# A hand-written order for a sort-attention kernel that feeds a maxout FFN: paired value sorts, groups of three PSUM tiles, other places for the loads

## The chip, the cores and the metric

The kernel runs on one core of one Trainium2 chip. The metric is the device time of one execution in microseconds (us), taken as the median of several runs. Times within one execution are read from a hardware profile of that execution, counted from its first instruction.

The engines are named as in the profile: PE is TensorE (matmuls; PEld its weight loads), DVE is VectorE, ACT is ScalarE, POOL is GpSimd, SP is SyncE. In this kernel POOL starts the loads from memory and SP starts the transposing DMAs and nearly all stores.

## The reference, cut to what matters

There are four items (B = 4), each with 8 heads, 768 positions and a head size of 64. The positions form 8 blocks of 96. An 8 by 8 matrix P for each item and head, made from `sort_net` by five Sinkhorn rounds, mixes the blocks of k and of v; attention then runs inside each block, and a maxout FFN follows on all 512 columns.

```python
for _ in range(5):                       # Sinkhorn
    P = exp(P - max(P, -1)); P /= sum(P, -1); P /= sum(P, -2)
k_sorted = einsum('bhij,bhjcd->bhicd', P, k_b)   # v_sorted alike
attn = softmax(scale * q_b @ k_sorted_b.T)       # within each block
x = (attn @ v_sorted_b)                          # -> (4*768, 8*64)
out = maximum(x @ w1, x @ w2) @ w_out            # (3072, 512), fp32
```

The maxout is computed as `relu(x (w1 - w2)) w_out + x (w2 w_out)`. So `w1` is replaced by the difference (four pieces, `w_difference`), and the product `wc = w2 w_out` is made once (`w2_transposes`, `w_product`). Once the differences are taken and w2 is transposed, w2 itself is not read any more.

## The kernel before, in words

Items are counted from one in this text (item one is `b = 0` in the code), steps within an item from 0.

**PSUM.** There is one pool of four tiles, each 128 x 1024 fp32 [...]. Every product of every kind takes a tile from it: `k_ps`, `v_ps`, `s_ps`, `o_ps`, `h_ps`, `out_ps`, `tq_ps`, `wc_ps`. A tile is handed out again when the instruction that reads it last has run, so a matmul group may have to wait for a copy on ACT or DVE.

**Steps of an item.** `load_k`, `load_v`, `load_q` (lines 132 to 161) start casting DMAs on POOL; each load instruction also waits for the landing of the eighth one before it. k and q come in buffers `k_raw` (two) and `q_raw` (one); v of two items lies in one buffer `v_raw`, one item in partitions 0 to 63 and the other in 64 to 127. `turn_v` reorders v into `v_dc`. `block_diagonals` spreads P into block-diagonal weights `bd`. Then:

- `sort_k(b, t)`, t = 0 to 2: 32 matmuls of 64 rows each into one PSUM tile, copied to `kT`.
- `sort_v(b, t)`, t = 0 to 3: 16 matmuls of 64 rows of one item, copied to `v_sb`. `sort_v_pair(b, t)`, t = 0 to 7: 16 matmuls, 8 for each of two items that lie in the two halves of the partitions; with this, two items take 8 tiles.
- `q_transposes`: item one and two by PE; later items are first laid in pairs (`pair_q`, DVE) and then transposed by two DMAs that SP issues.
- `scores(b, u)`, u = 0 to 7: 8 matmuls into one tile, then exp on ACT into one of 8 buffers `e`. u = 0, 1, 4, 5 need the first half of the transposed q, the others the second.
- `values(b, u)`: 8 matmuls of `e` with `v_sb`, then on DVE a reciprocal and a product that gives x.
- `x_transposes(b, t)`, t = 0 to 3, one for each two values steps: by PE for item one, by a DMA from SP (`xT`) for the others.

**The FFN of an item** is a list of units: 8 times `moe_h` (8 matmuls of 384 columns, then relu on ACT or DVE; the first four read transposes 0 and 1 of x, the last four 2 and 3), for item one 4 times `w_product`, and 12 times half an output tile (`moe_out`, 6 matmuls of 512 columns; four of them fill a PSUM tile, which is then copied and stored by SP).

**The order.** The program order of each engine is the order in which the Python code emits instructions. The start, to the end of item one's attention, is written by hand (lines 666 to 716), with matmuls on zeros (`keep_streaming`) at places where PE would stand still. In the loop (lines 743 to 805) the attention of item b+1 is woven into the units of item b: a dictionary `tail` gives some steps by hand, and the rest (`steps`) is spread evenly by the units' costs in the list `cost`. `pick` chooses ACT or DVE for a copy by a running estimate of their load.

Values are sorted so: item one alone, item two alone (`sort_v`), items three and four as a pair (`sort_v_pair`) in the FFN of item two. Scores are emitted in groups of two. The loads stand in the order v1 k1 q1 weights v2 k2, then (after three FFN units) q2 k3, later v3 v4 k4, q3, and q4 after q3 is laid in pairs.

Of the kernel before, what the change touches and what calls it, by code (L numbers as in the profile page):

```python
# [10 lines left out]
FP32 = mybir.dt.float32  # L11
BF16 = mybir.dt.bfloat16
# [4 lines left out]
def kernel(  # L17
# [112 lines left out]
        e_bufs.append(t)  # L130

    def load_q(b, by_pair=False):
        t = qpool.tile([128, H, R * D], BF16, tag="q_raw", name="q_raw", bufs=1)
        src = q[b].rearrange("h (p r) d -> p h (r d)", r=R)
        for hs in [slice(hp, H, HP) for hp in range(HP)] if by_pair else [slice(0, H)]:
            nc.gpsimd.dma_start(out=t[:, hs], in_=src[:, hs])  # L136
        q_raw[b] = t
# [13 lines left out]
                in_=k_src[b, :, ci * n : (ci + 1) * n],  # L151
            )

    def load_v(b, c0=0, pieces=2):
        r0 = (b % 2) * 64
        n = (BLK - c0) * D // pieces
        for m in range(pieces):
            nc.gpsimd.dma_start(
                out=v_raw[r0 : r0 + 64, c0 * D + m * n : c0 * D + (m + 1) * n],
                in_=v_src[b, :, c0 * D + m * n : c0 * D + (m + 1) * n],  # L160
            )

    w1_sb = big.tile([128, HP, DFF], BF16, tag="w1", name="w1_sb")
# [13 lines left out]
        c = slice(t0 * DFF // 4, t1 * DFF // 4)  # L177
        nc.gpsimd.dma_start(out=dst[:, :, c], in_=s[:, :, c])

    load_v(0, 0, 3)  # L180
    ident = const.tile([128, 128], BF16, tag="ident", name="ident")
    make_identity(nc, ident)
    load_k(0)
# [18 lines left out]

    w_difference(0, nc.gpsimd)
    w_difference(1, nc.gpsimd)
    load_v(1)
    load_k(1)


# [42 lines left out]


    id64 = const.tile([128, 64], FP32, tag="id64", name="id64")
    maskJ = const.tile([128, 6, NB], FP32, tag="maskJ", name="maskJ")
    maskM = const.tile([128, 2, 8], FP32, tag="maskM", name="maskM")

    def masks(part):
# [21 lines left out]
    sel_v, sel_k = {}, {}  # L279

    def selections(b):
        src = ident[0:G, b * 8 : b * 8 + 8]
        if b % 2 == 0:
            sel_v[b] = const.tile([G, 16, NB], BF16, tag=f"sel_v{b}", name="sel_v")
            nc.vector.tensor_copy(
                out=sel_v[b], in_=ident[0:G, b * 8 : b * 8 + 16].to_broadcast([G, 16, NB])
            )
        sel_k[b] = const.tile([G, 8, 16], BF16, tag=f"sel_k{b}", name="sel_k")
        nc.vector.tensor_copy(out=sel_k[b], in_=src.to_broadcast([G, 8, 16]))

    bd_v, bd_k = {}, {}

    def block_diagonals(kinds, m0=0):

        pe = ps_f32("pe")
        n = len(kinds)
        for c, (m, b) in enumerate(kinds):
            sel = (
                sel_k[b].rearrange("g h w -> g (h w)")
                if m  # L300
                else sel_v[b].rearrange("g h j -> g (h j)")
            )
            nc.tensor.matmul(
                pe[:, c * 64 : c * 64 + 64],
                sel,
                p_bf.rearrange("p i j -> p (i j)"),
                start=True,
                stop=True,
            )
        pm = const.tile([128, n, NB, NB], FP32, tag=f"pm{n}", name="pm")  # L310
        nc.vector.tensor_tensor(
            out=pm,
            in0=pe[:, 0 : n * 64].rearrange("p (m i j) -> p m i j", i=NB, j=NB),
            in1=maskJ[:, m0 : m0 + n].to_broadcast([128, n, NB, NB]).transpose([0, 1, 3, 2]),
            op=ALU.mult,
        )
        pt = const.tile([128, n, NB], FP32, tag=f"pt{n}", name="pt")
        nc.vector.reduce_sum(out=pt, in_=pm, axis=AX.X)
        for c, (m, b) in reversed(list(enumerate(kinds))):
            bd = const.tile([128, 8, NB], BF16, tag=f"bd{m}{b}", name="bd")  # L320
            nc.vector.tensor_tensor(
                out=bd,
                in0=maskM[:, m].to_broadcast([128, 8, NB]),
                in1=pt[:, c].to_broadcast([128, NB, 8]).transpose([0, 2, 1]),
                op=ALU.mult,
            )
            if m:
                bd_k[b] = bd.rearrange("p m i -> p (m i)")
            else:
                bd_v[b] = bd_v[b + 1] = bd.rearrange("p m i -> p (m i)")  # L330


    v_sb = big.tile([BLK, 128, D + 16], BF16, tag="v_sb", name="v_sb")
# [15 lines left out]
    def q_transposes(b, half, eng=None):  # L349
# [8 lines left out]
            )  # L358
            return
        ps = ps_bf16("tq_ps")  # L360
        if b == 0:
            nc.tensor.matmul(
                ps[:, 0:128], fill[:, 0:128], ident, is_transpose=True, start=True, stop=True
            )
# [44 lines left out]
    def sort_v(b, t, n=0, eng=None):  # L409
# [3 lines left out]
        for m in range(16):  # L413
# [8 lines left out]
        evac(  # L422
            v_sb[:, m0 : m0 + 64, t * 16 : (t + 1) * 16],
            ps[0:BLK].rearrange("p (d m) -> p m d", m=64),
            1024,
            eng=eng,
        )
# [235 lines left out]
        return SC, VA, TR  # L663

    first, second, both = slice(0, 64), slice(64, 128), slice(0, 128)
    keep_streaming(ps_f32("fill_ps"), 88 * 138, most=138)
    for it in range(5):
        sinkhorn(it)
        if it < 2:
# [9 lines left out]
    turn_v(first, "D", 80, 96)  # L679

    SC, VA, TR = att(0)
    sort_k(0, 0, 2048, "A")
    sort_k(0, 1, 0, "D")
    sort_k(0, 2, 0, "A")
    sort_v(0, 0, 0, "D")
# [2 lines left out]
    sort_v(0, 2, 0, "A")  # L688
    sort_v(0, 3, 0, "D")
    SC[0]()  # L690
    SC[1]()
    q_transposes(0, 1, "D")
    SC[4]()
    VA[0]()
    scores(0, 2, 1024)
    VA[1]()
    SC[3]()
    values(0, 2, 1024)
    x_transposes(0, 0, "A")
    values(0, 3, 512)  # L700
    SC[5]()
    moe_h_products(0, 0, 0, (0, 2), 512)
    x_transposes(0, 1, "A")
    VA[4]()
    SC[6]()
    moe_h(0, 0, 0, "A", (1, 3))
    SC[7]()
    VA[5]()
    moe_h(0, 0, 1, "A")
    x_transposes(0, 2, "A")  # L710
    VA[6]()
    w_difference(2)
    VA[7]()
    w2_transposes(0, "D")()
    w_difference(3)
    for b in range(1, B):
        selections(b)
    for c, n, m in [(2, 1, 0), (3, 3, 1)]:
        nc.vector.tensor_copy(
            out=maskJ[:, c : c + n],  # L720
            in_=maskJ[:, m].to_broadcast([128, NB, n]).transpose([0, 2, 1]),
        )
# [2 lines left out]
        turn_v(rows, "D", c0, c0 + 24)  # L725
        load["D"] += 850

    def load_rest():
        load_q(1)
        load_k(2)  # L730

    tail = {
        2: [TR[3], lambda: w2_transposes(1, "A")(), load_rest],
        4: [lambda: turn(second, 0)],
        5: [lambda: block_diagonals([(0, 2), (1, 1), (1, 2), (1, 3)], 2)],
        6: [lambda: turn(second, 24), lambda: turn(second, 48)],
        7: [lambda: turn(second, 72)],
        8: [lambda t=t: sort_k(1, t) for t in range(3)],
        9: [lambda: load_v(2), lambda: load_v(3), lambda: load_k(3)],
        14: [lambda: load_q(2)],  # L740
        18: [lambda: pair_q(2, 0), lambda: pair_q(2, 1), lambda: load_q(3)],
    }
    for b in range(B):
        units = [lambda t=t: moe_h(b, 0, t, None if b else "A") for t in range(4)]
        if b == 0:
# [13 lines left out]
        if b == B - 1:  # L759
# [1 line left out]
                lambda: moe_out_last(4, [(0, 512, "D")]),  # L761
                lambda: moe_out_last(5, [(0, 384, "D"), (384, 512, "A")]),
            ]
        steps, lo = [], 0
        if b < B - 1:
            qs = [lambda half=half: q_transposes(b + 1, half) for half in range(2)]
            ks = [lambda t=t, b=b: sort_k(b + 1, t) for t in range(3)]
            SC, VA, TR = att(b + 1)

            def group(*fs):  # L770
                return [lambda: [f() for f in fs]]

            if b == 0:
                lo = 9
                vs = [lambda t=t: sort_v(1, t) for t in range(4)]
                for m, c in enumerate((0, 24, 48, 72)):
                    VA[m + 1 : m + 2] = group(VA[m + 1], lambda c=c: turn(both, c))
                steps = group(*vs[0:2]) + group(vs[2], qs[0]) + group(vs[3], qs[1])
            elif b == 1:
                vs = [lambda t=t: sort_v_pair(2, t) for t in range(8)]  # L780
                tail[0] = qs
                tail[10] = [lambda: pair_q(3, 0), lambda: pair_q(3, 1)]
                steps = group(*ks) + group(*vs[0:2]) + group(*vs[2:4]) + group(*vs[4:6])
                steps += group(*vs[6:8])
            else:
                tail[0] = qs
                lo = 4
                steps = group(*ks)
            steps += group(*SC[0:2]) + VA[0:1] + group(*SC[2:4]) + VA[1:2] + group(VA[2], TR[0])
            steps += group(*SC[4:6]) + VA[3:4] + group(VA[4], TR[1]) + group(*SC[6:8]) + VA[5:6]  # L790
            steps += group(VA[6], TR[2]) + group(VA[7], TR[3])
        done = 0
        for n, unit in enumerate(units):
            elapse(100 * cost[n] if n < len(cost) else 0)
            unit()
            for step in tail.get(n, []):
                elapse(250)
                step()
            total = sum(cost[lo:])
            want = -(-len(steps) * sum(cost[lo : n + 1]) // total)  # L800
            while done < min(want, len(steps)):
                elapse(250)
                steps[done]()
                done += 1
        tail = {}
# [1 line left out]
_INS = ['q', 'k', 'v', 'sort_net', 'moe_w1', 'moe_w2', 'moe_w_out']  # L807
_OUTS = [((3072, 512), 'float32')]
# [25 lines left out]
```

## Time and profile before

| | |
|---|---|
| median of 5 runs | 170.65 us (170.15 to 171.35) |
| profiled execution | 170.15 us |
| its span, first to last instruction | 168.3 us |
| granted PE clock | 0.999 of full |
| PE busy | 160.7 us, 2000 matmuls |
| ACT busy / DVE busy | 85.7 us / 75.8 us |
| moved by DMA | 23.11 MB, mean 137 GB/s |
| largest groups | output products (line 617) 47.0 and 24.8 us; FFN products (590) 44.7 us; exp (469) 24.3 us |

Busy times of PE overlap, since matmuls are pipelined: a group's mean of 370 ns for 512 columns is longer than its share of the chain, in which consecutive ones take about 0.21 us each. A line of section 5 of the page gives the idle time ahead of a group and what ended it; a line of the chain in order of time gives start, length and what ran. Line 108 and 110 are the copy helper on ACT and DVE, line 82 the matmuls on zeros.

### The profile page before, as it was taken

To read this page: it belongs to the slowest core of one execution; us is meant where nothing else is said; L and a number is where in the kernel's file an instruction comes from. 1 tells how busy PE (TensorE), PEld (TensorE's weight loads), DVE (VectorE), ACT (ScalarE), POOL (GpSimd) and SP (SyncE) were. 2 spreads that over 40 slices of the span, in tenths; PEclk is the share of its full clock that TensorE was granted. 3 is DMA by queue.
4 is the path that set the end of the run, shared out by engine and by line. 5 is a ranking of instruction groups with operands and counts; after the bars stand their busy time and mean duration, and the time that the engine had idled before them with its cause. 6 is when DMAs were issued, how large, how long until landed. Compare 5 with 4: busy or idle time off the path is not lost.

```text
span 168.3 us, 4526 instructions
## 1 busy us (share of the span) xinstructions
PE 160.7 (96%) x2000; PEld 96.8 (58%) x2018; DVE 75.8 (45%) x174; ACT 85.7 (51%) x104; POOL 28.9 (17%) x44
## 2 busy tenths in 40 slices
PE   7999999999999999999999999999999999999991
PEld 7839667655764454566664545557545455654451
DVE  5978874957454458537734434205443160000011
ACT  3587878465673354176674504457605406642020
POOL 7857496233212004000000000000000000000000
PEclk9999999999999999999999999999999999999999
DMA  3999999999999994999700344590053255000333
GB/s 43 204 204 199 199 207 206 224 198 206 213 217 206 205 245 79 191 152 225 161 0 4 91 127 143 104 285 5 0 51 125 58 166 171 0 0 0 125 143 110
DMA packets 30243, 23.11 MB, mean 137 GB/s; under 512 B 16720, under 2 KB 25168, under 8 KB 30224
## 3 DMA queue, kind: packets, MB, share of 16 engines
q0 software_dynamic: 10880, 12.59, 44.7%
q1 hardware_dynamic: 19200, 10.17, 25.0%
q8 instruction: 16, 0.26, 0.6%
q10 hardware_dynamic: 144, 0.07, 0.1%
q14 instruction: 3, 0.02, 0.0%
HBM read 25.17 MB, written 6.29 MB: 187 GB/s over the span
## 4 chain that ended last, share of the span: by engine, by line
PE 86%; DVE 7%; issue 2%; ACT 2%; DMA 1%
PE out_ps L617 36%; PE h_ps L590 26%; PE o_ps L488 4%; PE wc_ps L570 4%; PE k_ps L394 4%; PE s_ps L461 4%; PE v_ps L415 2%; PE tq_ps L369 2%; PE v_ps L436 1%; DMA p_sb<-in_sort_net_dram 1%; PE tx_ps L526 1%; DVE colsum L243 1%; DVE p_sb L240 1%; ACT v_sb L108 1%; DVE rowsum L239 1%
## 5 line engine op out<-in xcount | busy, mean ns | idle before, releaser
L617 PE MATMUL out_ps<-wo_sb,g 128*128 128x512 bf16 (+2 forms) x188 | 47.0, 370 | 1.1 <-issue 0.3
L590 PE MATMUL h_ps<-xT,w_sb 128*128 128x384 bf16 x256 | 44.7, 326 | 0.6 <-ACT xT L108 0.4
L590 PEld LDWEIGHTS <-w_sb 128*128 128x128 bf16 x256 | 24.0, 98 | 16.4 <-DVE w_sb L194 0.4
L108 ACT COPY o<-out_ps 128x1024 f32<-128x1024 f32 x11 | 11.1, 1012 | 40.4 <-issue 22.8
L604 ACT ACTIVATE g<-h_ps 128x768 bf16<-128x768 f32 x27 | 21.9, 811 | 16.5 <-PE h_ps L590 16.5
L469 ACT ACTIVATE e<-s_ps 96x768 bf16<-96x768 f32 x32 | 24.3, 805 | 6.2 <-PE s_ps L461 6.2
L617 PEld LDWEIGHTS <-g 128*128 128x128 bf16 x200 | 16.9, 97 | 15.7 <-DVE x L505 0.4
L617 PE MATMUL out_ps<-wc,xT 128*128 128x512 bf16 (+2 forms) x100 | 24.8, 370 | 0.1
L505 DVE TENSOR_TENSOR x<-o_ps,rs 96x512 bf16<-96x512 f32 x32 | 22.0, 687 | 1.1
L499 DVE RECIPROCAL rs<-o_ps 96x8 f32<-96x8 f32 x32 | 6.5, 202 | 33.8 <-PE o_ps L488 33.6
L617 PEld LDWEIGHTS <-xT 128*128 128x128 bf16 x100 | 9.6, 97 | 11.2
L488 PEld LDWEIGHTS <-e 96*128 96x128 bf16 x256 | 11.7, 98 | 6.0 <-ACT e L469 0.2
L488 PE MATMUL o_ps<-v_sb,e 96*128 96x65 bf16 x256 | 12.9, 193 | 0.0
L652 DVE COPY o<-out_ps 128x512 f32<-128x512 f32 (+1 forms) x2 | 1.2, 624 | 25.0 <-PE out_ps L617 25.0
L110 DVE CAST kT<-k_ps 128x1024 bf16<-128x1024 f32 x5 | 6.0, 1223 | 12.3 <-PE k_ps L394 12.3
L110 DVE CAST v_sb<-v_ps 96x1024 bf16<-96x1024 f32 x8 | 9.6, 1215 | 2.6 <-PE v_ps L415 1.7
L108 ACT CAST v_sb<-v_ps 96x1024 bf16<-96x1024 f32 x8 | 8.0, 1005 | 3.3 <-PE v_ps L415 1.9
L461 PEld LDWEIGHTS <-kT 64*128 64x128 bf16 x256 | 6.1, 94 | 6.1 <-issue 5.2
L136 POOL DMA_DIRECT2D q_raw<-in_q_dram x7 | 6.4, 935 | 18.6 <-DVE rs L499 14.0
L461 PE MATMUL s_ps<-qT,kT 64*128 64x96 bf16 x256 | 8.9, 204 | 0.3 <-DVE qT L110 0.2
L82 PEld LDWEIGHTS <-fill 128*128 128x128 bf16 x98 | 7.4, 112 | 1.6 <-DVE fill L73 1.2
L606 DVE TENSOR_SCALAR g<-h_ps 128x768 bf16<-128x768 f32 x5 | 4.8, 958 | 7.3 <-PE h_ps L590 7.3
(77 smaller groups left out, 139.8 us busy)
## 6 DMA issues: line engine op xcount, KB each, us to landing
out_dram<-o SPq DMA_DIRECT2D x11, 512.0 KB, 3.0
k_raw<-in_k_dram POOLq DMA_DIRECT2D x12, 256.0 KB, 12.3
v_raw<-in_v_dram POOLq DMA_DIRECT2D x6, 384.0 KB, 12.8
q_raw<-in_q_dram POOLq DMA_DIRECT2D x3, 768.0 KB, 11.6
w_sb<-in_moe_w_dram POOLq DMA_DIRECT2D x4, 256.0 KB, 9.7
w_sb<-in_moe_w_dram POOLq DMA_DIRECT2D x2, 512.0 KB, 11.3
wo_sb<-in_moe_w_out_dram POOLq DMA_DIRECT2D x2, 512.0 KB, 14.7
v_raw<-in_v_dram POOLq DMA_DIRECT2D x3, 256.0 KB, 4.9
```

The lines of the kernel that those rows point to most:

```text
L82: nc.tensor.matmul(ps[:, 0:w], w0, fill[:, 0:w], start=True, stop=True)
L108: nc.scalar.copy(out=out_ap, in_=in_ap)
L110: nc.vector.tensor_copy(out=out_ap, in_=in_ap)
L394: nc.tensor.matmul(ps[r0 : r0 + 64, m * 64 : (m + 1) * 64], kv[r0 : r0 + 64, t * 16 + m, :], bd_k[b][r0 : r0 + 64, :], start=True, stop=True,)
L461: nc.tensor.matmul(ps[:, h2 * 512 + ii * 128 : h2 * 512 + ii * 128 + BLK], kT[b][rows, (hp * 8 + i) * BLK : (hp * 8 + i) * BLK + 128], rhs ...
L469: nc.scalar.activation(out=e[:, 0 : 8 * BLK].rearrange("p (t c r) -> p t c r", t=8, r=R), in_=ps[0:BLK] .rearrange("p (t f) -> p t f", t=8 ...
L488: nc.tensor.matmul(ps[:, h2 * 512 + ii * 65 : h2 * 512 + (ii + 1) * 65], e[:, (h2 * 4 + ii) * BLK : (h2 * 4 + ii) * BLK + 128], v_sb[:, m0 ...
L505: nc.vector.tensor_tensor(out=x, in0=ov[:, :, :, 0:D], in1=rs.to_broadcast([BLK, 2, 4, D]), op=ALU.mult,)
L570: nc.tensor.matmul(ps[:, 0:512], w2T[:, fb, dmt * 128 : (dmt + 1) * 128], wo_sb[:, fb, :], start=(fb == 0), stop=(fb == NFB - 1),)
L590: nc.tensor.matmul(h_ps[t][:, m * 512 : m * 512 + TCH], w1_sb[:, hp, fb * 128 : (fb + 1) * 128], xT[:, b % 2, ch, hp % 2, hp // 2, :], sta ...
L604: nc.scalar.activation(out=g, in_=src, func=AF.Relu)
L617: nc.tensor.matmul(dst, g_tiles[b, ch, m // 2][:, m % 2, off : off + 128] if m < NFB else xT[:, b % 2, ch, hp % 2, hp // 2, off : off + 12 ...
```

## The change

- **Value sorts.** Item one is still sorted alone. Items two and three are now the pair (`sort_v_pair(2, ...)` in the FFN of item one), and item four is sorted by a new function, `sort_v_halved`: its v is loaded twice, into both halves of the partitions, and 16 matmuls of one tile work on 8 columns of d from one half and 8 from the other, so that it takes 4 tiles. The block diagonals and selections follow: five block diagonals in one call instead of four, `maskJ` with 7 rows instead of 6, `sel_v` written by two small copies instead of one.
- **Order.** The even spreading is gone; three dictionaries list all steps by hand. Scores and value sorts are mostly in groups of three PSUM tiles.
- **Loads.** After weights: k2, q2, v2 and v3 in four interleaved pieces, k3. q3 goes into the tile of w2, once w2 is not read any more. v4 (twice), k4 and q4 are placed later in the program, v4 behind the turns of v2 and v3, k4 and q4 in the FFN of item two.
- **The start.** Score 4 stands before score 1 and before the second half of q; values 3 and 4 to 6 move up by one place; five of ten zero matmuls of 512 columns go (the train of small ones at the very start becomes 86 of 142 columns instead of 88 of 138); the third weight difference stands before values 7; the second w2 transposes stand behind the fourth FFN unit.

```diff
 def load_q(b, by_pair=False):
-        t = qpool.tile([128, H, R * D], BF16, tag="q_raw", name="q_raw", bufs=1)
+        if b == 2:
+            t = w2_sb.rearrange("p t f -> p (t f)")[:, 0 : H * R * D].rearrange(
+                "p (h x) -> p h x", h=H
+            )
+        else:
+            t = qpool.tile([128, H, R * D], BF16, tag="q_raw", name="q_raw", bufs=1)
...
-    load_v(1)
     load_k(1)
...
+    def sort_v_halved(b, t, eng=None):
+        m0 = (b % 2) * 64
+        ps = ps_f32("v_ps")
+        for m in range(8):
+            for par in range(2):
+                rows = slice(par * 64, par * 64 + 64)
+                nc.tensor.matmul(
+                    ps[:, par * 512 + m * 64 : par * 512 + (m + 1) * 64],
+                    v_weights(rows, par * 32 + t * 8 + m),
+                    bd_v[b][rows, :],
+                    start=True,
+                    stop=True,
+                )
...
-    sort_k(0, 0, 2048, "A")
+    sort_k(0, 0, 1024, "A")
...
     SC[0]()
+    SC[4]()
+    q_transposes(0, 1, "D")
     SC[1]()
-    q_transposes(0, 1, "D")
-    SC[4]()
     VA[0]()
-    scores(0, 2, 1024)
-    VA[1]()
+    SC[2]()
+    values(0, 1, 512)
     SC[3]()
-    values(0, 2, 1024)
+    values(0, 2, 512)
     x_transposes(0, 0, "A")
-    values(0, 3, 512)
+    VA[3]()
+    VA[4]()
     SC[5]()
...
+    load_q(1)
+    for piece in range(2):
+        for b in (1, 2):
+            load_v(b, which=piece)
+    load_k(2)
...
+    first_tail = {
+        2: [lambda: x_transposes(0, 3)],
+        3: [lambda: w2_transposes(1, "A")(), lambda: load_q(2)],
+        5: [lambda: block_diagonals([(0, 2), (0, 3), (1, 1), (1, 2), (1, 3)], 2)],
+        7: KS,
+        9: [TQ[0], TURN[0]],
+        10: [SC[0], TQ[1], TURN[1]],
+        11: SC[1:4] + TURN[2:4] + [lambda half=half: load_v(3, half=half) for half in range(2)],
+        12: VS[0:3],
+        13: VS[3:6],
+        14: VS[6:8] + [SC[4]],
+        16: [VA[0], lambda: pair_q(2, 0), VA[1]],
+        17: SC[5:8] + [TR[0]],
+        18: [VA[2], lambda: pair_q(2, 1)],
+        19: [VA[3], TR[1]],
+        20: [VA[4]],
+        21: [VA[5], TR[2]],
+        22: [VA[6], VA[7], TR[3]],
+    }
...
+    second_tail = {
+        0: [lambda: q_transposes(2, 0), lambda: q_transposes(2, 1)],
+        2: KS,
+        4: SC[0:3],
+        5: [VA[0]],
+        6: [VA[1], lambda: load_k(3), lambda: load_q(3)],
+        7: [VA[2], TR[0]],
+        8: SC[3:6],
...
+        13: SC[6:8] + VS[0:1],
...
+        16: VS[1:4],
+        17: [lambda: pair_q(3, 0)],
+        18: [lambda: pair_q(3, 1)],
+    }
```

The numbers in the dictionaries are units of the FFN of items one, two and three; a step stands behind its unit. `third_tail` has the attention of item four in the same manner, with scores in groups of 3, 3 and 2.

## The prediction

> **What bounds the kernel now.** I read the page first: shares of busy time, then the slices, then the chain.
>
> ```profile
> PE 160.7 (96%) x2000; PEld 96.8 (58%) x2018; DVE 75.8 (45%) x174; ACT 85.7 (51%) x104; POOL 28.9 (17%) x44
> ...
> DMA  3999999999999994999700344590053255000333
> ...
> PE 86%; DVE 7%; issue 2%; ACT 2%; DMA 1%
> ```
>
> TensorE is 96% busy and is 86% of the chain that ends last, so a matmul saved is time saved and a wait of PE is time lost. The second row is as important: the DMA engines are full from the second slice to about the twentieth (4.2 us each, so to about 80 us), with short breaks at 62 to 69 us.
>
> Then the chain in order of time, for what PE pays per step:
>
> ```profile
> 72.28 1.30 PE h_ps L590 x8
> 73.58 1.64 PE k_ps L394 x96
> 75.22 1.41 PE h_ps L590 x8
> 76.62 0.57 PE v_ps L436 x32
> ...
> 84.64 0.45 PE s_ps L461 x16
> 85.09 2.71 PE h_ps L590 x16
> ```
>
> An FFN unit of 8 matmuls costs 1.30 us, but 1.41 ahead of a sort: 0.11 for entering half-array work. Elsewhere in the chain one score tile alone is 0.28 and two are 0.45, so a tile is 0.17 and a group has 0.11 of its own; with the entry, a group costs some 0.2 beyond its tiles. Two paired value tiles are 0.57, so 0.24 each.
>
> Third, the trace in order of time for the only stretch where a load runs beside the transposes that SP issues:
>
> ```profile
> 65.59 1.77 POOL L136 DMA_DIRECT2D q_raw<-in_q_dram  x1 [14.00 <-DVE rs L499]
> ...
> 68.89 4.93 SPq L518 DMA_TRANSPOSE xT<-x  x2
> ...
> 74.57 6.92 SPq L355 DMA_TRANSPOSE qT<-q_pair  x2
> ```
>
> The view of tile xT in 68 to 73.8 us says of the two transposes there:
>
> ```profile
> DMA to landing us min/median/max: 6.3/7.6/8.8
> ```
>
> and of those in 91 to 110 us, where nothing is loaded:
>
> ```profile
> DMA to landing us min/median/max: 2.7/2.8/3.1
> ```
>
> A transpose of x takes 2.8 us from issue to landing alone, and up to 8.8 when it meets the load of q of item four (issued 65.6, landed 11.6 later, at 77.2). Before, that costs nothing: it hits transposes 3 and 4 of item two, not needed until 81.2.
>
> [...]
>
> **The change part by part**, against the profiled execution (170.15 us, span 168.3), in its clock.
>
> Fills: 5 of 10 zero matmuls of 512 columns after the Sinkhorn go (0.21 each in a run). They stood in front of waits that stay: block diagonals on DVE (ready 12.45), qT copy (19.9), xT copy (25.2). Bounds 0 to -1.1; I take 0, as PE then waits for the same copies. One selection copy (0.27) becomes two of half size in the Sinkhorn chain: +0.1.
>
> Start of item one: values step 6 (steps are counted from 0, items from one) now comes ahead of the second FFN unit, so DVE does its reciprocal and product (0.9) by 27.5, and the third weight difference (0.69) is done at 28.3 instead of 30.1. PE was held by it until 30.15; it is now free at about 29.45. With the second w2 transposes behind the fourth unit, output products begin some 0.9 sooner, apart from the sorts. Take -0.9 (0 to -1.2).
>
> Value sorts: before, item two alone 1.51 + 0.57, items three and four in four groups of 0.57, and 6 entries of 0.11: 5.0. After, items two and three in 8 tiles and three groups, item four in 4 half-depth tiles with one group of its own: 12 x 0.24 + 4 x 0.2 = 3.7. So -1.3.
>
> Scores: 12 groups become 10, and two of those stand beside a value sort with no new entry: -0.6.
>
> PSUM waits. Before, PE lost 0.6 around 56 to 66 us (q_pair copies and turns ahead of x on DVE; 0.26 at 66.19). They go: -0.6. New ones: the third value tile needs the slot of score 3, whose exp ends third on ACT (50.05 + 0.8 + 0.75 + 0.75 = 52.35, PE ready 51.9): +0.5. Score 7 of item two needs the slot of values 1, whose x stands behind q_pair (0.55) on DVE: ready 62.25, PE 61.85: +0.5. The FFN unit behind each first score group waits for the copy of g: +0.1 twice. Together +1.2.
>
> PE's sum: 0 + 0.1 - 0.9 - 1.3 - 0.6 - 0.6 + 1.2 = -2.1; walking the slots through the three output stretches step by step gives -2.6. I take -2.4.
>
> Loads, the part not on PE. Order after: k2, q2, v of two and three in four pieces, k3, q3 (into the spent w2 tile), v of four into both partition halves (twice the bytes), k4, q4. Each waits only for its buffer and for the eighth load before it (q3 also for the last w2 transposes, 33.3 us), so "late" in the program isn't late on the queue: POOL has nothing else to do. V of four waits for the turns (49.4 us), k4 for the sort at 40.5, q4 for the q transposes at 47.6, all past before the queue gets there. From 43.6 to 62.3 us (landings of q2 and q3) five items of 768 KB landed: 3.74 us each. From wo's landing at 32.7, at 3.7 each: k2 36.4, q2 40.1, v 47.5, k3 51.2, q3 54.9, v of four twice 62.3, k4 66.0, q4 69.7. First needs (38.9, 44.0, turns with values at 51.4) are met.
>
> But now there is no break. By 69.7 these share the engines: output 1 (DVE copy done 59.6), transpose 1 of item two (x done 62.3), output 2 (66.4), transpose 2 (66.6). The windows of before give their work: 0.28 x 3.7 = 1.0 us for a lone transpose, 0.46 x 3.0 = 1.4 for an output. All done at 69.7 + 2 x 1.4 + 2 x 1.0 = 74.5, and transpose 2, last in its queue, lands about 75.7. Item two's first FFN unit is reached at 71.8 by the sum above and its third matmul needs transpose 2 at 72.1. Wait: 3.6 us (between 0, if transposes are served first, and 5, if it lands at 77 as before). Everything on PE is behind it. Before, transposes 1 and 2 flew in the break, 3.9 and 2.8 us.
>
> Late next: qT of item three, issued after output 3 at about 73.5, behind transposes 3 and 4: 74.5 + 2.0 + 1.4 + 3.9 (both qT by the window at 108.9) = 81.8, landed about 83. Score 2 is now in the first group and needs the second half; unhindered PE would be there at 80.5, with the 3.6 at 84. So it costs nothing more, but caps what can be saved at the earlier place: without the first wait this one still takes up to 2.5.
>
> Sum: -2.4 + 3.6 = +1.2. The profiled execution would be 171.35; it stands 0.5 below the median of five (170.65), so the forecast is 171.8.
>
> **The rivals.** (a) Transposes get through: they land by 72.5 and qT by 81, as a plain 512 KB output overlapped q3's end at 61 us at even turns. Then PE's sum holds, less what qT takes back: 168.1 to 169.8, take 168.6. It ends on the other side; it decides where transpose 2 lands before about 73.6. Against it: 8.8 us at 68.9. (b) The wait is about as large as the saving (1.6 to 3.2): 169.8 to 171.5, no change. For it: loads could run a little faster than 3.7. (c) More than that: PSUM groups of three cost double (1.2 more) or transpose 1 is late too: 173.5. The program does contain the paired sorts; that the pair runs side by side is seen in before (0.57 for 32), so "the change does nothing" isn't kept.
>
> **How the numbers follow.** Forecast (171.5 to 173.0) 0.42, (c) 0.09, (b) 0.24, (a) 0.25. A difference of 0.5% (0.85 us) is about what a measurement of this kernel can tell from none. Faster is (a), 0.25; same is (b), 0.24; slower the rest, 0.51. The range leaves out the best fifth of (a) and the worst of (c): 168.4 to 173.4; the forecast alone has 170.9 to 173.0.
>
> **What would show it.** Right: PE idle 2 to 5 us at the first FFN unit of item two, released by the transpose of x, near 72 to 76 us; xT landings of 8 us or more there; DMA slices at 9 with no break at 62 to 69; value sorts of 48 in about 0.83; sum of PE busy some 3 us less. Wrong: those transposes landing within 5 us, no PE gap over 1 us between 70 and 85; or a wait instead at the first score group of item three (qT), or gaps at 36 to 52 us because v or q came late.

## The result, and the profile after

The changed kernel takes 171.68 us in the median of 22 runs (171.13 to 174.34); the kernel before, on the same chips, 170.58 us. The ratio of the two is 1.0074, 95% interval 1.0053 to 1.0094: 1.1 us slower, where 171.8 was forecast. Seven of the 22 runs lie at 173.2 to 174.3 and the others at 171.1 to 172.1, and the profiled execution (174.19 us, span 172.0) is one of the long ones, for a reason seen below.

The page of the kernel after, with the rows that were shown of before (engine, busy us, share of the span; then tenths by slice; then the chain's shares), and the group of FFN products (busy us, mean ns, idle time ahead of them and what ended it):

```profile
PE 159.6 (93%) x1994; PEld 96.4 (56%) x2011; DVE 78.6 (46%) x181; ACT 83.8 (49%) x102; POOL 29.1 (17%) x46
...
PEclk9999999999999999987999999999999999999999
DMA  3999999999999999999102253384021753000332
...
PE 79%; DVE 7%; DMA 6%; ACT 4%; issue 3%; ACTq 0%
...
L621 PE MATMUL h_ps<-xT,w_sb 128*128 128x384 bf16 x256 | 46.2, 334 | 3.4 <-DMA xT<-x 2.6
```

Three things are new. DMA has no break any more: 9 from the second to the nineteenth slice (4.3 us each), where before had a 4 at 63 to 67 us. DMA is now 6% of the chain. And PE's clock row has an 8 and a 7 at the end of that stretch.

The chain in order of time (start, us, what) gives the place:

```profile
66.48 1.26 PE out_ps L648 x6
67.74 7.92 DMA xT<-x
75.66 0.04 issue
75.70 5.42 PE h_ps L621 x22
```

The second transpose of item two is issued at 67.7 us and takes 7.9 us. The trace in order of time shows PE there (in brackets: idle time before, and what ended it):

```profile
72.61 0.48 PE L621 MATMUL h_ps<-xT,w_sb 128*128 128x384 bf16 x2
75.70 1.28 PE L621 MATMUL h_ps<-xT,w_sb 128*128 128x384 bf16 x4 [2.61 <-DMA xT<-x]
```

PE reaches item two's FFN at 72.61, does the two products that need the first transpose only, and stands for 2.61 us. Four products then take 1.28 us, where four take 0.81 or 0.82 at full clock. The view of tile xT in 62 to 74 us says of the four transposes:

```profile
DMA to landing us min/median/max: 4.1/6.9/9.6
```

The clock in three windows around it (us, PE busy and matmuls, granted clock, DMA share, GB/s):

```profile
72.50:75.70 3.20, 0.59 (x3) 1.00 1.21 204
75.70:79.10 3.40, 3.40 (x12) 0.53 1.11 285
79.10:81.10 2.00, 2.00 (x14) 0.95 1.85 203
```

After the wait PE runs at half clock for 3.4 us (granted 0.50 in 75.9 to 79.3 us). That costs this execution 1.7 us on top of the wait, an estimate (half of 3.4).

To see where PE's own time went, I cut the kernels into stretches by what PE starts. A: from item one's first key sort to the first product of w2 and w_out, without item two's key sort (1.64 us), which stands elsewhere before. B: from there to item two's first FFN unit, with that sort. C and D: on to the first FFN units of items three and four. Starts are from the trace in order of time, for example A of after is 40.99 - 12.52 - 1.64.

| us | A | B | C | D | sum |
|---|---|---|---|---|---|
| before | 27.06 | 32.57 | 34.67 | 32.00 | 126.30 |
| after (profiled execution) | 26.83 | 33.26 | 37.76 | 31.98 | 129.83 |
| e1, loads held back | 26.66 | 33.13 | 33.80 | 31.98 | 125.57 |
| e4, zeros in the wait | 27.07 | 33.13 | 35.48 | 31.97 | 127.65 |
| e5, e1 and qT early | 26.83 | 33.13 | 33.32 | 31.98 | 125.26 |
| e9, e1 with the old start | 27.45 | 33.13 | 34.15 | 31.98 | 126.71 |
| e10, all mends | 26.90 | 32.66 | 33.32 | 31.98 | 124.86 |

### The profile page after: what moved, and what is told of

Same layout as the page of the kernel before. It is cut to its first block, busy times and chain, and to the rows that moved or that the text cites. A ratio compares the mean times of both kernels' runs of the same rounds, so it can differ in the third digit from the quotient of the medians.

```text
span 172.0 us, 4529 instructions
## 1 busy us (share of the span) xinstructions
PE 159.6 (93%) x1994; PEld 96.4 (56%) x2011; DVE 78.6 (46%) x181; ACT 83.8 (49%) x102; POOL 29.1 (17%) x46
## 4 chain that ended last, share of the span: by engine, by line
PE 79%; DVE 7%; DMA 6%; ACT 4%; issue 3%; ACTq 0%
PE out_ps L648 32%; PE h_ps L621 26%; DMA xT<-x 5%; PE wc_ps L601 4%; PE k_ps L402 4%; PE o_ps L519 3%; PE s_ps L492 2%; PE tq_ps L377 2%; PE v_ps L467 1%; PE tw_ps L582 1%; ACT e L500 1%; ACT g L635 1%; PE v_ps L423 1%; ACT xT L108 1%; DMA p_sb<-in_sort_net_dram 1%
## 5 line engine op out<-in xcount | busy, mean ns | idle before, releaser
L621 PE MATMUL h_ps<-xT,w_sb 128*128 128x384 bf16 x256 | 46.2, 334 | 3.4 <-DMA xT<-x 2.6
L648 PE MATMUL out_ps<-wo_sb,g 128*128 128x512 bf16 (+2 forms) x187 | 46.0, 370 | 1.5 <-issue 1.1
L621 PEld LDWEIGHTS <-w_sb 128*128 128x128 bf16 x256 | 24.8, 99 | 20.6 <-issue 5.6
L635 ACT ACTIVATE g<-h_ps 128x768 bf16<-128x768 f32 x28 | 22.7, 810 | 21.9 <-PE h_ps L621 21.8
L108 ACT COPY o<-out_ps 128x1024 f32<-128x1024 f32 x9 | 9.1, 1013 | 27.3 <-PE out_ps L648 22.7
L110 DVE CAST kT<-k_ps 128x1024 bf16<-128x1024 f32 x6 | 7.2, 1221 | 16.8 <-PE k_ps L402 16.8
L637 DVE TENSOR_SCALAR g<-h_ps 128x768 bf16<-128x768 f32 x4 | 3.8, 956 | 11.3 <-PE h_ps L621 11.3
L163 POOL DMA_DIRECT2D v_raw<-in_v_dram x11 | 5.9, 539 | 12.8 <-DVE v_dc L221 7.6
```

Source lines behind the costliest of these rows:

```text
L108: nc.scalar.copy(out=out_ap, in_=in_ap)
L110: nc.vector.tensor_copy(out=out_ap, in_=in_ap)
L621: nc.tensor.matmul(h_ps[t][:, m * 512 : m * 512 + TCH], w1_sb[:, hp, fb * 128 : (fb + 1) * 128], xT[:, b % 2, ch, hp % 2, hp // 2, :], sta ...
L635: nc.scalar.activation(out=g, in_=src, func=AF.Relu)
L648: nc.tensor.matmul(dst, g_tiles[b, ch, m // 2][:, m % 2, off : off + 128] if m < NFB else xT[:, b % 2, ch, hp % 2, hp // 2, off : off + 12 ...
```

## The experiments

Theory: the change saves PE time, but puts the loads of item four beside the transposes of item two, and the wait for the second of these costs more. Rival: PE's own work got no cheaper, and the wait only shows it.

**Loads held back (e1).** POOL, which issues the loads in order, gets a one-column copy of an FFN result ahead of them:

```diff
+    gate = const.tile([128, 1], BF16, tag="gate", name="gate")
+
+    def hold_loads(b, ch, t):
+        nc.gpsimd.tensor_copy(out=gate, in_=g_tiles[b, ch, t][:, 0, 0:1])
...
-        4: SC[0:3],
-        5: [VA[0]],
-        6: [VA[1], lambda: load_k(3), lambda: load_q(3)],
+        4: [lambda: hold_loads(1, 1, 0)] + SC[0:3],
+        5: [VA[0], lambda: load_k(3), lambda: load_q(3)],
+        6: [VA[1]],
```

> The changed kernel, with the loads of item four's keys and queries (1.5 MB) held back on POOL until the fifth FFN unit of item two has been copied, so that they run at about 80 us instead of 63 to 75. Theory (loads delay the second transpose of item two, and the 2.6 us of PE wait that follow hide a real saving on PE): transposes of x then land within about 4 us as in the kernel before, the PE wait at the first FFN unit of item two is under 0.5 us, time 168.2 to 169.4 us, faster than both kernels (170.6 and 171.7). Rival (the saving on PE is not there: groups of three PSUM tiles cost what the merged sorts save, and the wait is only where this shows): 171 to 172 us with or without the wait. Second rival (a wait at qT of item three takes its place): 170 to 171 us, and a PE wait near 80 us released by qT.

169.92 us; ratio to before 0.9975 (0.9949 to 1.0001). The page, and the view of tile xT in 62 to 75 us:

```profile
PE 160.6 (95%) x2011; PEld 97.3 (58%) x2011; DVE 78.5 (47%) x181; ACT 83.8 (50%) x102; POOL 29.7 (18%) x47
...
DMA  3999999999999983649699936192022653000333
```

```profile
DMA to landing us min/median/max: 2.8/3.2/3.5
```

The transposes take 2.8 to 3.5 us instead of 4.1 to 9.6, the wait at the FFN is gone, and 1.75 us with it. The theory's place and cause stand. Its size doesn't: 168.2 to 169.4 was expected, faster than both kernels, and the interval still reaches the time of before. The view of PE's waits names a part of what is missing:

```profile
PE s_ps L492 <- DMA qT<-q_pair: 0.6, 1, 0.6
```

It is the second rival, in small: score 2 of item three waits for qT. The rest of the shortfall is in PE's own saving: even with that 0.64 us taken off, e1's stretches sum to 124.93, 1.4 us less than before and not 2.4.

**Half of item four's values loaded once (e2).**

```diff
-    ... + [lambda half=half: load_v(3, half=half) for half in range(2)],
+    ... + [lambda: load_v(3, half=1)],
```

> The changed kernel with the first of the two loads of item four's values left out (half of the columns of that item's values are then those of item three; no PE, DVE or ACT instruction is removed). 0.77 MB, some 3.7 us of DMA, less ahead of the second transpose of item two. Theory: that transpose lands 2.5 to 3.7 us sooner, at 72 to 73 us, the PE wait falls from 2.6 to under 0.6 us, time 168.5 to 169.6 us. Rival (PE's own work is the cause): 171 to 172 us.

170.00 us; ratio 0.9975 (0.9950 to 1.0000). The second transpose lands at 71.3 us instead of 75.7, no PE wait at the FFN, 0.6 us at qT. So it isn't the hold itself, and not only the loads of q and k: 768 KB less of another load ahead of that transpose (an estimated 3.7 us, by the time that an item of this size took in before) does it as well. The time is again above the expected range, by 0.4 us. The same trace shows the first two groups of three value tiles, the first with a wait for a PSUM tile in it:

```profile
52.20 1.13 PE L467 MATMUL v_ps<-bd,v_dc 64*128 64x64 bf16 x48
54.66 0.88 PE L467 MATMUL v_ps<-bd,v_dc 64*128 64x64 bf16 x48
```

**More load (e3).**

```diff
+    def more_load():
+        nc.gpsimd.dma_start(out=w2_sb[:, 3, :], in_=k_src[3, :, 0:DFF])
...
-    ... + [lambda half=half: load_v(3, half=half) for half in range(2)],
+    ... + [lambda half=half: load_v(3, half=half) for half in range(2)] + [more_load],
```

> The changed kernel with one more load of 512 KB (a piece of item four's keys into unused columns, about 2.5 us of DMA at 3.7 us for 768 KB) ahead of item four's keys. No work is left out and no other instruction changes. Theory: the second transpose of item two lands about 2.5 us later (near 78), the PE wait grows from 2.6 to about 5 us, time 173.8 to 174.8 us, more if PE then runs at half clock as it did after the wait in the changed kernel's profile. Rival: under 0.5 us of change, since loads that only shift a transpose already overlapped would not be what sets the time: 171.5 to 172.2 us.

173.71 us in four runs, just under the expected range; ratio 1.0142 (1.0059 to 1.0224). The dose was smaller than I wrote: the profile counts a key piece of this shape as 256 KB, so by the same rate it is an estimated 1.2 us of DMA and not 2.5. The second transpose lands at 76.46 instead of 75.66, 0.8 us later, and the waits of PE grow from 2.6 to

```profile
PE h_ps L621 <- DMA xT<-x: 3.4, 2, 2.9
```

The direction is as expected; the size is 0.8 us for 1.2 us more of loads. In this trace, too, PE runs at about half clock after the wait (granted 0.54 and 0.61 in 76 to 78 and 78 to 80 us), and four runs (172.5 to 174.4) are too few to tell the price of the wait from that of the clock.

**Zeros in the wait (e4).**

```diff
+        if b == 1:
+            units[0] = lambda: moe_h(1, 0, 0, n=5120)
```

> The changed kernel with ten matmuls of zeros, 512 columns each (about 2.1 us), put into the PSUM tile of item two's first FFN unit ahead of its products: they lie in the wait for the second transpose. Theory (the wait is for a transfer, and the half clock that followed it in the profile comes from PE standing idle): time 171.3 to 171.9, as the changed kernel's common case, and no execution at 173 to 174 us; PE clock in the profile stays full after 75 us. Rival (PE work is what bounds there): 2 us more, 173.5 to 174.

171.65 us, ratio 1.0062 (1.0044 to 1.0080); one run of 20 at 173.0, where none was expected and after has seven of 22 at 173.2 and above. The trace in order of time, and windows of PE with columns as above:

```profile
72.75 2.32 PE L82 MATMUL h_ps<-fill 128*128 128x512 bf16 x10
74.91 4.06 PE L621 MATMUL h_ps<-xT,w_sb 128*128 128x384 bf16 x24
```

```profile
74.00:76.00 2.00, 2.00 (x12) 1.00 1.11 249
76.00:78.00 2.00, 2.00 (x15) 1.00 2.03 260
```

Ten more matmuls take 2.16 us of PE (72.75 to 74.91) and leave the time as it was, so the place is a wait for a transfer. The clock stays full in this trace (1.00 in both windows). That the idle time brings the half clock fits, but low clocks come without it too: by my estimate 3.4 us at half clock make the mean clock of an execution about 0.99 (1 - 1.7/172), and a mean of 0.991 or less is found in six of the 22 of after, in one of the 20 of e4, and in two, one and one of the 20 each of e1, e2 and e5, which have no such wait.

In this execution the second transpose landed at 74.59 us, 0.3 before the zeros ended. So its stretch C (35.48, against 33.80 in e1) holds 2.16 us of zeros and no wait for it. Of these, 0.5 come back at the first scores of item three: there e1 waits 0.64 for qT, which has landed in e4, where only the next FFN unit waits, 0.28 for the copy of g (the relu output of an FFN unit). C is thus 1.7 us longer than in e1, as the times are (171.65 - 169.92). The wait itself varies: without the zeros it would here have been some 1.5 us, an estimate from two products of 0.16 us each after 72.75 and the landing at 74.59, and not 2.6.

Then the question was where the rest of PE's saving went, 1.0 us by e1. The next runs start from e1.

**qT early (e5).** The transposes of item three's q pair are issued ahead of item one's last output:

```diff
-        22: [VA[6], VA[7], TR[3]],
+        22: [VA[6], VA[7], TR[3]]
+        + [lambda half=half: q_transposes(2, half) for half in range(2)],
...
-        0: [lambda: q_transposes(2, 0), lambda: q_transposes(2, 1)],
```

> The kernel of run e1_hold (loads of item four's keys and queries held back), with the two transposes of item three's query pair issued on SP ahead of the last output of item one instead of behind it (about 73 instead of 75 us). Theory (score 2 of item three waits 0.56 us for the second half of qT, as the profile with the loads held back shows, and nothing else is late): that wait goes, item three's FFN begins 0.5 us sooner, time 0.3 to 0.6 us under e1_hold's 169.9: 169.3 to 169.6. Rival (the transposes of x, whose third is needed at 81 us, are what qT now delays): the same wait at the fifth FFN unit of item two, no change.

169.61 us, ratio 0.9954 (0.9933 to 0.9975). The wait for qT is gone and stretch C is 0.48 us shorter. What is left there is a wait of 0.28 for the copy of g behind the group of three scores.

**Score order (e6).**

```diff
     SC[0]()
-    SC[4]()
-    q_transposes(0, 1, "D")
     SC[1]()
+    q_transposes(0, 1, "D")
+    SC[4]()
```

> The kernel of run e1_hold with the start of item one in the score order of before: scores 0, 1, second half of q, scores 4. Theory (scores 4 ahead of scores 1 put the exp of scores 1 third on ACT, so that values 1 begin at 20.7 us instead of 20.3, which is why the second FFN unit of item one begins at 27.1 us and not at 26.5, and why 0.9 us were not saved in the start of item one but 0.3): values 1 begin near 20.3 us, the second FFN unit of item one 0.3 to 0.5 us sooner, time 169.4 to 169.7. Rival (the second half of q, 0.1 us later, or the copies of x take it back): start of item one the same within 0.1 us, 169.9.

169.82 us, ratio 0.9976 (0.9958 to 0.9995): a miss. Stretch A is 26.91, no shorter than e1's 26.66, and values 1 still begin at 20.74 us:

```profile
19.72 0.34 PE L492 MATMUL s_ps<-qT,kT 64*128 64x96 bf16 x8 [0.43 <-DVE qT L110]
20.51 0.39 PE L82 MATMUL o_ps<-fill 128*128 128x512 bf16 x1 [0.44 <-PE s_ps L492]
```

The exp of scores 1 is not what holds them. The matmul of zeros ahead of them needs no exp, and it stands 0.44 us for nothing but a step of PE's own that is long done.

**Fills back (e7).**

```diff
-    sort_k(0, 0, 1024, "A")
+    sort_k(0, 0, 2048, "A")
...
-    SC[2]()
+    scores(0, 2, 1024)
...
-    values(0, 2, 512)
+    values(0, 2, 1024)
```

> The kernel of run e1_hold with the five matmuls of zeros (512 columns) that the change takes out of item one put back: two before the first key sort, two at scores 2, one at values 2. The forecast has them at 0 (they lie in front of waits that stay; bounds 0 to 1.1 us): time 169.9 within 0.2 us, and item one's second FFN unit begins within 0.1 us of 27.1. Rival (they are on the path): up to 1.1 us more, 170.4 to 171.0.

169.62 us in seven runs, ratio 0.9940 (0.9906 to 0.9973), not apart from e1's. Stretch A is 26.71 (41.47 - 13.12 - 1.64) against 26.66. The five matmuls cost nothing; so does taking them out. What its time is under e1's lies in stretch C (33.36 against 33.80), where the wait for qT is 0.2 us and not 0.6.

**Groups of two (e8).**

```diff
-        5: SC[0:3],
+        5: SC[0:2],
...
+        7: SC[2:4],
         8: [VA[1]],
         9: [VA[2], TR[0]],
-        10: SC[3:6],
+        10: SC[4:6],
```

> The kernel of run e1_hold with the first two score groups of item four, of three PSUM tiles each, made into three of two tiles. The forecast's price (0.2 us for a group beyond its tiles, less 0.1 for the FFN unit that waits for the copy behind a group of three): 0.1 to 0.3 us slower, seen in the stretch from item three's first FFN unit to item four's (31.97 us with groups of three, 32.00 in the kernel before). Rival, from that stretch: nothing, since the FFN unit that stands 0.28 us behind a group of three gives it back: within 0.1 us, 169.9.

169.78 us, ratio 0.9965 (0.9951 to 0.9980), and stretch D is 31.88 (138.40 - 106.52): 0.1 us shorter than with groups of three. The rival holds. The trace of e8, and then of e1, where the first group of item four ends:

```profile
116.15 0.51 PE L492 MATMUL s_ps<-qT,kT 64*128 64x96 bf16 x16
116.60 1.47 PE L621 MATMUL h_ps<-xT,w_sb 128*128 128x384 bf16 x8
```

```profile
116.41 0.68 PE L492 MATMUL s_ps<-qT,kT 64*128 64x96 bf16 x24
117.37 0.81 PE L621 MATMUL h_ps<-xT,w_sb 128*128 128x384 bf16 x4 [0.28 <-ACT g L635]
```

A pair is left at once; behind a group of three the FFN unit waits 0.28 us for its PSUM tile. What one entry fewer saves (about 0.1 us by the chain of before, 1.41 against 1.30), this wait takes.

**The old start (e9).** Item one's order of before, on e1, with as many matmuls of zeros as after has (excerpt):

```diff
-    VA[4]()
     SC[5]()
     moe_h_products(0, 0, 0, (0, 2), 512)
     x_transposes(0, 1, "A")
+    VA[4]()
     SC[6]()
-    VA[5]()
     moe_h(0, 0, 0, "A", (1, 3))
     SC[7]()
-    VA[6]()
+    VA[5]()
     moe_h(0, 0, 1, "A")
     x_transposes(0, 2, "A")
+    VA[6]()
     w_difference(2)
     VA[7]()
-    w2T_ready = w2_transposes(0, "D")
+    w2_transposes(0, "D")()
     w_difference(3)
-    w2T_ready()
```

> The kernel of run e1_hold with item one's order of before: scores 0, 1, second half of q, scores 4; values 4, 5 and 6 back behind their old neighbours; the second w2 transposes back behind the third FFN unit; the same five matmuls of zeros as the changed kernel has. The forecast's step (the start of item one is worth 0.9 us): 170.7 to 170.9, and the products of w2 and w_out begin 0.9 us later (28.3 us after the first key sort in e1_hold, 27.1 in the kernel before, where the key sort of 1.64 us is not yet among them). Rival, from the profiles so far: worth 0.2 to 0.4 us, time 170.1 to 170.3.

170.55 us, ratio 1.0007 (0.9980 to 1.0033): 0.6 us more than e1, between the two theories. The wait for the third weight difference is back, in the trace in order of time:

```profile
30.47 0.82 PE L621 MATMUL h_ps<-xT,w_sb 128*128 128x384 bf16 x4 [0.25 <-DVE w_sb L199]
```

But stretch A is then 27.45, 0.4 more than before has with the same order. So the new order is worth 0.6 us, and something else that came with the change takes back 0.4. The trace of e9 and then of the kernel before at 20 us:

```profile
19.81 0.33 PE L492 MATMUL s_ps<-qT,kT 64*128 64x96 bf16 x7
20.50 0.21 PE L492 MATMUL s_ps<-qT,kT 64*128 64x96 bf16 x1 [0.36 <-issue]
```

```profile
19.92 0.46 PE L461 MATMUL s_ps<-qT,kT 64*128 64x96 bf16 x8 [0.21 <-DVE qT L110]
20.31 0.42 PE L488 MATMUL o_ps<-v_sb,e 96*128 96x65 bf16 x8
```

In e9 PE stands inside a score step, between its seventh and eighth matmul, where the program has no wait. In e10 it is between the fourth and the fifth, in e1, e6 and after ahead of the zeros. Counted in matmuls and weight loads, it is the same place in PE's stream in every kernel with the change: after 702 of them in the traces of twelve, after 701 in that of after, which lacks some records. The one that follows is called row 703 here.

What PE stands ahead of it lengthens stretch A in full. In nine traces with five matmuls of zeros and the new order (after, e1 to e6, e8, e11) the stand is 0.19 to 0.61 us and stretch A 26.66 to 27.07, and A less the stand is 26.46 or 26.47 in all nine. That e6 is among them shows again that its score order is worth nothing. For e9 the difference is 27.09 (27.45 - 0.36), so that the new order is worth 0.62 us.

**All mends (e10), and without the five fills (e11).** e5, e7 and one swap, so that score 7 of item two doesn't wait for an x behind the q copy:

```diff
-        16: [VA[0], lambda: pair_q(2, 0), VA[1]],
+        16: [VA[0], VA[1], lambda: pair_q(2, 0)],
```

> Loads held back, qT of item three ahead of item one's last output, the five matmuls of zeros back, and the copy of item three's first q pair behind values 1 of item two instead of between values 0 and 1, so that score 7 of item two doesn't wait 0.34 us for the x of values 1. Theory (the gains add up where each wait is on PE): 0.3 us under e5_qt_early and e7_fills_back (169.6): 169.1 to 169.4, the fastest of all, and no PE wait over 0.3 us between 20 and 110 us. Rival (another wait takes the place of each): 169.6.

> The same as e10_best with the changed kernel's five matmuls of zeros alone. If the five others are worth nothing, as the forecast has it: the same as e10_best within 0.15 us. If they fill waits at no cost and keep something ready on PE, as run e7_fills_back could be read (169.6 against 169.9): 0.2 to 0.3 us slower than e10_best.

e10: 168.80 us, ratio 0.9895 (0.9859 to 0.9931), below the range expected. e11: 168.90 us, ratio 0.9908 (0.9879 to 0.9937). Both beat both kernels by more than their intervals, 1.7 to 1.8 us under before and 2.8 to 2.9 under the change as it was. The five zeros make 0.1 us between the medians, which is not clear of noise. The swap takes 0.47 us out of stretch B. The page of e10:

```profile
PE   7999999999999999999999999999999999999991
...
DMA  3999999999999984659499936290023494000333
```

The loads thin out again where the transposes fly (from about 60 us), and PE's slices are 9 from the second to the last but one.

**Rows of PE's stream (e12).**

```diff
-    keep_streaming(ps_f32("fill_ps"), 86 * 142, most=142)
+    keep_streaming(ps_f32("fill_ps"), 88 * 138, most=138)
```

> A look at the first 22 us alone. The kernel of run e10_best with the matmuls of zeros before the Sinkhorn's third step as in the kernel before: 88 of 138 columns instead of 86 of 142 (68 columns fewer in all, but four more rows in PE's stream of instructions). The transposes of x and q of items two to four by DMA are plain copies of the same bytes here, so those items' results are not the reference's, and times after 60 us and in all say nothing; up to there every engine's work is e10_best's. In every kernel with the change PE goes on past the 703rd row of its stream (matmuls and weight loads counted together) at 20.5 to 21.0 us, 1.3 to 1.45 us after a 16 KB packet of the instruction queue ended, after standing 0.2 to 0.6 us; in the kernel before that packet begins at 17.6 instead of 18.1 to 18.7 us and the stand is 0.1 us. Theory (the packet is asked for when PE's stream passes a fixed row, which the four rows less have put behind the wait for p_bf at 11.3 us): packets near 10.8 and 17.6 us again, row 704 at 20.2 us or before. Rival (the packets come by time or by other traffic): packets at 11.9 and 18.1 us or later, row 704 at 20.5 us or later.

Between the two. The packets begin at 11.72 and 17.82 us (e10: 11.86 and 18.22; before: 10.75 and 17.61), and PE goes on at 20.25 us (e10: 20.49). The first packet did not go back to 10.8, so the fixed row of the theory is not shown. The second is 0.4 us earlier than in e10, but only 0.14 earlier than in e2 (17.96), so one execution doesn't tell an effect of the four rows from scatter. In each, PE goes on 1.3 to 1.7 us after the packet's end.

## Why the prediction was right, and where it was not

The total was right, 171.8 against 171.7, and so was its cause. Its two large terms were both too large. PE's saving was put 1.4 us too high (2.4 forecast; 1.0 in e5, which waits for neither transfer), and the wait 1.5 us too high (3.6 forecast; 2.1 by the times of after and e5, 171.68 - 169.61). The errors cancel: that the total is right to 0.1 us is luck.

- **What bounds the kernel.** Right: a PE wait that an experiment took away came out of the time, less what the next wait took (e1 1.75 of 2.6 us, e5 0.3 to 0.5 of 0.6).
- **Loads.** Landings forecast and measured: k2 36.4 and 36.2, v 47.5 and 48.7, k3 51.2 and 51.8, q3 54.9 and 55.7, v of four 62.3 and 63.1, k4 66.0 and 68.3, q4 69.7 and 75.0. The last two were forecast without the outputs and transposes beside them and put together with these to 74.5, an estimate from windows of before; q4 landed at 75.0 and transpose 2 at 75.66, where 75.7 was said. So close a match is partly chance: in e4's execution the two land at 72.7 and 74.6. The experiments on both sides show that it is the loads: transpose 2 lands at 71.3 with less of them (e2) and at 76.46 with more (e3).
- **The wait.** 3.6 forecast; 2.6 in the trace of after, which is a long execution, and 2.1 by the times against e5. The transfer was placed rightly; PE was there at 72.6 and not at 71.8. Against e1 the wait is worth only 1.7, since e1 pays at qT instead. The forecast named this cap, with up to 2.5 us; it measured 0.64 in e1's trace, of which e5 gets back 0.48.
- **Fills.** 0 forecast; e7 and e11 against e10 give 0 to 0.1.
- **Start of item one.** This step failed in part: 0.9 forecast, 0.2 in stretch A. The mechanism was right, and e9 sizes it at 0.6. The other 0.4 came with the change beside it; 0.25 of that is the longer stand ahead of PE's row 703, for which the forecast had no term (0.36 in e9 and in after, about 0.1 before: 0.46 for eight score matmuls that take 0.34 elsewhere). The rest is not located.
- **Value sorts.** 5.0 to 3.7 forecast; the groups of before sum to 4.9 (half of the unpaired 4.4, which is item one's, left out, and 2.7 of the paired), those of e1 to 3.9 (2.6 and 1.3), with 0.2 of the wait at the third tile in it, which is counted below. Without it they are nearly as forecast. Stretch B, which takes on the pair, is 0.56 us longer in e5, and C, which loses it, 1.35 shorter.
- **Scores.** This step fell: 0.6 forecast for fewer and larger groups, nothing measured at item four (e8). An FFN unit ahead of half-array work does take 0.11 longer in the chain of before (1.41 against 1.30), but a group of three leaves the next FFN unit waiting 0.28 for a PSUM tile, not 0.1.
- **PSUM waits.** The three places are those named: 0.25 at the third value tile (a group of 48 takes 1.13 us in e2 with the wait and 0.88 at the next), 0.34 at score 7, 0.28 at each of two FFN units. Sum 1.15, forecast 1.2. The split was off, the sum was not.
- **PE's sum.** -2.4 forecast; e5, which has neither wait for a transfer, gives 125.26 - 126.30 = -1.0. The terms that make the difference: start 0.7, score groups 0.4 to 0.6, and the 0.3 that I added to the sum of the parts because the step-by-step walk gave more. I took a figure between two estimates of my own, 2.1 and 2.6, without a reason for it.
- **Signs.** The PE gap, the landings (9.6 and 7.9 us for the first two transposes) and the full DMA slices came as named; groups of 48 value matmuls take 0.88, near the 0.83 that was said, where they don't wait. The drop of some 3 us in PE's busy time did not come: 160.7 before, 159.6 after, with 3.4 us at half clock in it, and 160.6 in e1. Busy times overlap and hold some waits (in e2 48 value matmuls take 1.13 us with one and 0.88 without), so this was a poor sign.
- **Rival (a)** needed transposes that get through; they do when the loads are held back (2.8 to 3.5 us in e1), and then the time is 169.9, not the 168.6 written. It takes the mends of e10 to get there.

## What to carry to other kernels

When an edit brings loads forward, look for the small transfers that used to fly in the break: here 1.5 MB loaded 32 to 46 us before it was needed cost 1.7 us, and one dummy copy on the issuing engine gave it back. A saving on the bounding engine is worth only what the next wait leaves (here 1.75 us of a wait of 2.6, in e1): price the wait behind each larger group as well as the entry that it saves. And when a forecast has both a saving and a wait, take the wait from where the engine will really arrive, with the later waits that it hides.

## What the runs showed of the hardware

**Half clock after a short wait.** In the trace of after PE stands for 2.61 us, to 75.70, and the granted clock is 0.50 from 75.9 to 79.3 us, so 3.4 us. In that of e3 it stands for 2.9 us, and the clock is 0.54 in 76 to 78 us and 0.61 in 78 to 80, by my estimate the same 3.4 us at half (0.46 and 0.39 of 2 us, doubled). With ten matmuls of zeros in the wait, e4's trace has 1.00 from 74 to 78 us, and mean clocks of 0.991 or less are rarer (one of 20 executions against six of 22). How long a wait it takes, and what sets the length of the slow stretch, these traces don't show.

**A stand at one row of PE's stream.** In the changed kernel and in all the kernels built on it PE goes on with row 703 at 20.25 to 21.0 us, 1.3 to 1.7 us after the end of a 16 KB packet of the queue that the profile calls "instruction", whatever work stands there (in the trace of after the packet takes 18.08 to 19.06 us and PE goes on at 20.50). The stand is 0.2 to 0.6 us, and stretch A is longer by all of it. The kernel before has that packet at 17.6 us, the others at 17.8 to 18.7, and loses 0.1. That PE waits for the packet is my guess from this timing, not shown, and what sets the packet's time stays open.
